# A last product with its weights stationary: the output of an MLP made transposed and turned by VectorE

## The chip, the cores and the metric

The kernel runs on one core of a Trainium2 chip. The metric is the device time of one execution in microseconds; for a kernel it is the median of its runs. Beside it stands one profiled execution, from which all rows below are read.

## The reference

The inputs `u`, `v` (4 x 3072 x 256) and `z` (4 x 3072 x 64) pass three stages; all arrays are float32.

```python
scores = (1.0 / S) * np.matmul(z, z.transpose(0, 2, 1))
attn_out = u * np.matmul(np.maximum(scores, 0.0) ** 2, v)
x_prev = np.concatenate([zeros((B, 1, D)), x[:, :-1]], axis=1)   # x = attn_out
xk = mu_k * x + (1.0 - mu_k) * x_prev
xr = mu_r * x + (1.0 - mu_r) * x_prev
k = np.maximum(xk @ w_k, 0.0)                  # 256 -> 1024
x2 = sigmoid(xr @ w_r) * (k * k @ w_v)         # 1024 -> 256
h = np.maximum(x2 @ w_in, 0.0)                 # 256 -> 2048
out = (h * h) @ w_out                          # 2048 -> 256, 12288 tokens
```

## The kernel before

Every float32 product is made of three matmuls on float32r parts: an operand is split into a high part (the value cast) and a low part (the rest), and high x high, low x high and high x low are summed in PSUM. The helper `split` (lines 80 to 85) makes the parts: the cast on ScalarE or VectorE, the subtraction on VectorE.

The first part, `attention`, takes some 1000 us. It makes the attention output for 24 blocks of 512 tokens and leaves it transposed (features on partitions, tokens along the columns) in DRAM, and between its steps it converts and stages the weights. The second part, `channel_mix_and_mlp`, goes over the 24 token blocks (`NBLK`), and it is the part that the change touches. Its order of work is written out by hand: for each of the 16 hidden chunks `f` of 128 features of a block (`NF2`), `up2` of the next chunk, a piece of the next block's first MLP (`up1`, `down1`, `gate_r`, from the table `before`), then `down2(n, f)`, then what the tables `after` and `aside` put there (mixing, gating, the load of a later x). After the sixteenth chunk comes `store(n)`. Each engine runs its instructions in this order, and so does SP with its transfers.

`up` (line 203) makes six matmuls for one chunk: 128 x 128 weights stationary, 512 tokens moving, three products for each half of the 256 inputs. ScalarE then takes relu and square (lines 157 and 158), VectorE the cast and the subtraction (84 and 85). `down1` (lines 218 to 222) also keeps the weights stationary: two accumulators of [128 features, 512 tokens], six matmuls a chunk.

`down2` (lines 524 to 533) does it the other way. The activations of 128 tokens are stationary, four times a chunk, and the weights move: once 512 columns (high and low part of `w_out` side by side, line 530), once 256 columns (the low part of the activations times the high part of the weights, line 532). The output then has tokens on partitions. It lies in four PSUM tiles `o0` to `o3` of one bank each, in one buffer; in each the second half collects the two small products. `store` adds the halves (ScalarE copies one, line 540, VectorE adds, line 541), and one transfer a block writes 512 KB (line 545; two of half the size in the last block). `split_piece` splits the pieces of `w_in` and `w_out` during the first block.

PSUM has eight banks: two for `ps_v`, four for `ps_o`, two for `ps_u`, whose two tiles `ups` are written by `up` and freed by the relu.

Of the kernel before, what the change touches and what calls it, by code (L numbers as in the profile page):

```python
# [7 lines left out]
F32 = mybir.dt.float32  # L8
F32R = mybir.dt.float32r
U32 = mybir.dt.uint32  # L10
AF = mybir.ActivationFunctionType
ALU = mybir.AluOpType
PSUM = bass.MemoryType.PSUM
DRAM = bass.MemoryType.DRAM

P = 128
Q = 32
T = 512
# [3 lines left out]
def tile_relu2_attention__rwkv_channel_mix__relu2_mlp(  # L22
# [18 lines left out]
    nc = tc.nc  # L41
    B, S, D = u.shape
# [3 lines left out]
    ND = D // P  # L46
    NJ = S // P
    NB = S // T
    NBLK = B * NB
    NF1 = F1 // P  # L50
    NF2 = F2 // P


    HS = 2.0**32
    G = 4
# [9 lines left out]
    raw_p = ctx.enter_context(tc.tile_pool(name="raw", bufs=3))  # L65
# [14 lines left out]
    def split(hi, lo, src, on_act=False):  # L80
        if on_act:
            nc.scalar.copy(hi, src)
        else:
            nc.vector.tensor_copy(hi, src)  # L84
        nc.vector.tensor_tensor(out=lo, in0=src, in1=hi, op=ALU.subtract)  # L85

    raws = {}
# [6 lines left out]
    def split_raw(key, hi, lo):  # L94
        split(hi, lo, raws.pop(key), True)
# [65 lines left out]
    def relu2_split(ps, scale):  # L161
        hi, lo = parts(*pools["hidden"])
        split(hi, lo, relu2(ps, scale))
        return hi, lo
# [32 lines left out]
    def up(lhs, rhs, f):  # L197

        ps = pools["ps"].tile([P, T], F32, tag="w", name="ups")
        k = 0  # L200
        for h, m in ((0, 0), (1, 0), (0, 1)):
            for c in range(ND):
                nc.tensor.matmul(ps, lhsT=lhs(h, c, f), rhs=rhs[:, m, c, :],  # L203
                                 start=k == 0, stop=k == 3 * ND - 1)
                k += 1
        return ps

    def up1(n, f):
        ps = up(lambda h, c, f: wk[:, h, c, f * P:(f + 1) * P], xk_t[n], f)
        kt[n, f] = relu2_split(ps, 1.0)  # L210
# [16 lines left out]
    def load_piece(i):  # L227
        if i < len(w_pieces):
            src = w_pieces[i][0]
            load_raw(("w32", i), src, src.shape[1], src.shape[2])  # L230
# [265 lines left out]
    def channel_mix_and_mlp():  # L496
        with ExitStack() as st:
            wp = st.enter_context(tc.tile_pool(name="wp", bufs=1, reuse_waits="tile"))
            ps_o = st.enter_context(tc.tile_pool(name="ps_o", bufs=1, space=PSUM, reuse_waits="tile"))
            ps_w = st.enter_context(tc.tile_pool(name="ps_u", bufs=2, space=PSUM, reuse_waits="tile"))  # L500
            win = [wp.tile([P, 2, ND, T], F32R, name=f"win{i}") for i in range(F2 // T)]
            wout = [wp.tile([P, G, 2, D], F32R, name=f"wout{i}") for i in range(NF2 // G)]
            pools["ps"], pools["hidden"] = ps_w, (wp, "h", 6)
            gt, acc_o, x2, sig = {}, {}, {}, {}

            def gate_r(n, d):
                ps = up(lambda h, c, f: wr[:, h, c, f * P:(f + 1) * P], xr_t[n], d)
                t = wp.tile([P, T], F32, tag=f"sig{d}", name="sig")
                nc.scalar.activation(out=t, in_=ps, func=AF.Sigmoid)
                sig[n, d] = t  # L510

            def gate_v(n, d):
                if d == 0:
                    x2[n] = wp.tile([P, 2, ND, T], F32R, tag="x2", name="x2", bufs=2)
                t = el.tile([P, T], F32, tag="a", name="x2f")
                nc.vector.tensor_tensor(out=t, in0=acc_v[n][d], in1=sig.pop((n, d)), op=ALU.mult)
                split(x2[n][:, 0, d, :], x2[n][:, 1, d, :], t)

            def up2(n, f):
                q, r = divmod(f, T // P)  # L520
                ps = up(lambda h, c, f: win[q][:, h, c, r * P:(r + 1) * P], x2[n], f)
                gt[n, f] = relu2_split(ps, HS)

            def down2(n, f):
                if f == 0:
                    acc_o[n] = [ps_o.tile([P, 2, D], F32, tag=f"o{c}", name=f"o{c}") for c in range(G)]
                hi, lo = gt.pop((n, f))
                w = wout[f // G]
                for c in range(G):
                    nc.tensor.matmul(acc_o[n][c], lhsT=hi[:, c * P:(c + 1) * P], rhs=w[:, f % G, :, :],  # L530
                                     start=f == 0, stop=False)
                    nc.tensor.matmul(acc_o[n][c][:, 1, :], lhsT=lo[:, c * P:(c + 1) * P], rhs=w[:, f % G, 0, :],  # L532
                                     start=False, stop=f == NF2 - 1)

            def store(n):
                y = raw_p.tile([P, G, D], F32, tag="raw", name="y")
                a = acc_o.pop(n)
                for c in range(G):
                    t = wp.tile([P, D], F32, tag="yc", name="yc", bufs=4)
                    nc.scalar.mul(t, a[c][:, 1, :], HS**-2)  # L540
                    nc.vector.scalar_tensor_tensor(out=y[:, c, :], in0=a[c][:, 0, :], scalar=HS**-2, in1=t,
                                                   op0=ALU.mult, op1=ALU.add)
                    if c == G - 1 or n == NBLK - 1 and c % 2:
                        c0 = c - 1 if n == NBLK - 1 else 0
                        nc.sync.dma_start(out=out[n * T + c0 * P:n * T + (c + 1) * P, :].rearrange("(c p) d -> p c d", p=P),
                                          in_=y[:, c0:c + 1])

            def split_piece(i):
                _, cs, fs = w_pieces[i]
                if i % 2 == 0:  # L550
                    t = win[fs.start // T]
                    split_raw(("w32", i), t[:, 0, cs], t[:, 1, cs])
                else:
                    t = wout[cs.start // G]
                    split_raw(("w32", i), t[:, :, 0, fs], t[:, :, 1, fs])
                load_piece(i + AHEAD)

            before, after, aside = {}, {}, {}  # L560
            for f, unit, a in ((0, up1, 2), (1, down1, 1), (2, up1, 3), (3, down1, 2), (4, up1, 4), (5, down1, 3),
                               (6, up1, 5), (7, down1, 4), (8, up1, 6), (9, down1, 5), (10, gate_r, 0),
                               (11, gate_r, 1), (12, down1, 7)):
                before[f] = (1, unit, a)
            after[9] = (1, up1, 7)
            after[10] = (1, down1, 6)
            before[13], before[14] = (2, up1, 0), (2, up1, 1)
            before[15] = (2, down1, 0)
            aside[1], aside[2] = (1, mix, 1, 0), (1, mix, 1, 1)
            aside[3] = (2, load_x)  # L570
            aside[7], aside[9] = (2, mix, 0, 0), (2, mix, 0, 1)
            aside[12], aside[13] = (1, gate_v, 0), (1, gate_v, 1)
            assert NF1 == 8 and NF2 == 16

            def run(n, what):
                if what and n + what[0] < NBLK:
                    what[1](n + what[0], *what[2:])

            gate_r(0, 0)
            gate_v(0, 0)  # L580
            split_piece(0)
            gate_r(0, 1)
            gate_v(0, 1)
            split_piece(1)
            up1(1, 0)
            up1(1, 1)
            up2(0, 0)
            up1(1, 2)
            for n in range(NBLK):
                last = n == NBLK - 1  # L590
                for f in range(NF2):
                    if f == 0 and last:
                        up2(n, 1)
                    ahead = n * NF2 + f + (2 if last else 1)
                    if ahead < NBLK * NF2:
                        up2(*divmod(ahead, NF2))
                    run(n, before.get(f) if n or f else (1, down1, 0))
                    down2(n, f)
                    run(n, after.get(f))
                    run(n, aside.get(f))  # L600
                    if n == 0 and f % 4 < 2 and f // 4 < 3:
                        split_piece(2 + f // 4 * 2 + f % 4)
                store(n)

    with tc.manual_schedule():
        attention()
        channel_mix_and_mlp()
# [29 lines left out]
```

## Time and profile before

| | |
|---|---|
| median of 3 runs | 2641.64 us (2640.64 to 2646.01) |
| the profiled execution | 2645.41 us, span 2643.6 us |
| TensorE busy | 2609.6 us, 99% of the span |
| VectorE busy | 1765.4 us, 67% |
| ScalarE busy | 1523.5 us, 58% |
| mean granted TensorE clock | 0.997 |

Busy times of TensorE come from records that overlap, since matmuls are pipelined and their ends are modelled: 99% says that something was always under way, not that the array was always full. The shares are means over the whole program. From about 1010 us on only the second part runs; there VectorE and ScalarE are busy for some 55% and 50% of the time.

### The profile page before, as it was taken

What the parts mean: (1) busy time and instruction counts of PE and PEld (TensorE: products, weight loads), DVE (VectorE), ACT (ScalarE), POOL (GpSimd) and SP (SyncE); (2) the same over time, 40 slices, a digit from 0 to 9 for tenths busy, and PEclk for the clock granted to TensorE, in tenths of its full rate; (3) what the DMA queues carried; (4) which work ended last, traced back from release to release, by engine and by line L of the source; (5) the groups of instructions that cost most, each with busy time, mean ns of one, the idle gap of its engine ahead of it and who ended that gap; (6) DMA issues with size and microseconds to landing.
All of it is one profiled execution on the core that took longest, in us unless ns stands there. A gap on an engine that the chain in (4) does not pass through costs nothing.

```text
span 2643.6 us, 33655 instructions
## 1 busy us (share of the span) xinstructions
PE 2609.6 (99%) x12096; PEld 2167.0 (82%) x12096; DVE 1765.4 (67%) x3118; ACT 1523.5 (58%) x2571; POOL 0.2 (0%) x4
## 2 busy tenths in 40 slices
PE   7999999999999999999999999999999999999999
PEld 6887888788788888888888888888888888888887
DVE  8887888888888886555555555555555555555554
ACT  8766876776577665454445554544544444455454
POOL 0000000000000000000000000000000000000000
PEclk9999999999999999999999999999999999999999
DMA  7687678776876752000000000000000000000000
GB/s 191 166 210 175 181 199 193 189 212 174 219 215 167 223 156 64 17 17 17 17 17 17 17 17 17 10 16 17 17 17 9 17 17 17 17 17 16 17 9 17
DMA packets 262952, 218.75 MB, mean 83 GB/s; under 512 B 160128, under 2 KB 190848, under 8 KB 259712
## 3 DMA queue, kind: packets, MB, share of 16 engines
q1 hardware_dynamic: 262784, 216.60, 30.2%
q8 instruction: 94, 1.54, 0.2%
q14 instruction: 74, 0.61, 0.1%
HBM read 124.28 MB, written 92.27 MB: 82 GB/s over the span
## 4 chain that ended last, share of the span: by engine, by line
PE 92%; DVE 3%; DMA 2%; SPq 1%; issue 1%; ACT 1%; DVEq 0%; ACTq 0%
PE ups L203 32%; PE o L530 13%; PE v L375 8%; PE v L371 8%; PE v L372 8%; PE o L532 7%; PE v L219 3%; PE v L222 3%; PE v L218 3%; PE sps L344 2%; PE sps L343 2%; DMA mixed<-turned 2%; SPq L245 1%; DVE alo L353 1%; DMA zn<-in_z_dram 1%
## 5 line engine op out<-in xcount | busy, mean ns | idle before, releaser
L157 ACT ACTIVATE a<-ups 128x512 f32<-128x512 f32 x576 | 344.1, 597 | 794.1 <-PE ups L203 778.2
L84 DVE CAST hhi<-a 128x512 fp32r<-128x512 f32 x568 | 242.2, 426 | 661.5 <-ACT a L158 646.0
L203 PE MATMUL ups<-x,win 128*128 128x512 f32 x2304 | 593.8, 393 | 0.5 <-DVE x L84 0.5
L158 ACT ACTIVATE a<-a 128x512 f32<-128x512 f32 x912 | 576.6, 632 | 29.1
L530 PE MATMUL o<-wout,hhi 128*128 128x512 f32 x1536 | 556.4, 397 | 0.0
L203 PEld LDWEIGHTS ups<-x,win 128*128 128x128 f32 x2304 | 408.6, 188 | 86.6 <-DVE x L84 0.9
L371 PE MATMUL v<-ahi,vhl 128*128 128x512 f32 x1152 | 451.3, 392 | 6.5 <-ACT ahi L338 6.4
L372 PE MATMUL v<-ahi,vhl 128*128 128x512 f32 x1152 | 451.0, 391 | 3.4 <-DVE vhl L278 3.4
L532 PE MATMUL o<-wout,hlo 128*128 128x256 f32 x1536 | 430.6, 280 | 0.0
L85 DVE TENSOR_TENSOR hlo<-a,hhi 128x512 fp32r<-128x512 f32 x568 | 393.5, 693 | 49.7 <-DVE hhi L84 2.3
L375 PE MATMUL v<-alo,vhl 128*128 128x512 f32 x1152 | 359.6, 394 | 12.4 <-DVE alo L353 12.2
L530 PEld LDWEIGHTS o<-wout,hhi 128*128 128x128 f32 x1536 | 288.8, 188 | 66.1
L532 PEld LDWEIGHTS o<-wout,hlo 128*128 128x128 f32 x1536 | 290.2, 189 | 14.8
L203 PE MATMUL ups<-mixed,wk 128*128 128x512 f32 x1152 | 292.9, 390 | 0.0
L375 PEld LDWEIGHTS v<-alo,vhl 128*128 128x128 f32 x1152 | 215.5, 189 | 65.2 <-DVE alo L353 20.3
L371 PEld LDWEIGHTS v<-ahi,vhl 128*128 128x128 f32 x1152 | 217.3, 189 | 54.6 <-ACT ahi L338 8.8
L372 PEld LDWEIGHTS v<-ahi,vhl 128*128 128x128 f32 x1152 | 217.6, 189 | 49.0 <-DVE vhl L278 3.7
L203 PEld LDWEIGHTS ups<-mixed,wk 128*128 128x128 f32 x1152 | 214.7, 188 | 45.3
L157 ACT ACTIVATE a<-sps 128x512 f32<-128x512 f32 x336 | 199.4, 594 | 81.4 <-PE sps L344 74.1
L314 DVE STREAM_TRANSPOSE turn<-a 128x512 f32<-128x512 f32 x240 | 207.9, 866 | 22.0 <-ACT a L158 21.6
L353 DVE TENSOR_TENSOR alo<-a,ahi 128x512 fp32r<-128x512 f32 x336 | 221.5, 664 | 0.0
L338 ACT CAST ahi<-mixed 128x512 fp32r<-128x512 f32 x220 | 132.2, 619 | 152.9 <-PE v L372 75.5
(69 smaller groups left out, 2281.5 us busy)
## 6 DMA issues: line engine op xcount, KB each, us to landing
turned<-turn SPq DMA_DIRECT2D x60, 1024.0 KB, 5.1
mixed<-turned SPq DMA_DIRECT2D x220, 256.0 KB, 5.3
raw<-in_v_dram SPq DMA_DIRECT2D x24, 512.0 KB, 5.2
u<-in_u_dram SPq DMA_DIRECT2D x192, 64.0 KB, 4.2
xT<-uT SPq DMA_DIRECT2D x48, 256.0 KB, 3.4
out_dram<-y SPq DMA_DIRECT2D x23, 512.0 KB, 2.9
x<-xT SPq DMA_DIRECT2D x20, 513.0 KB, 3.8
zn<-in_z_dram SPq DMA_DIRECT2D x96, 64.0 KB, 4.2
```

Of the source, the lines that this page charges most:

```text
L84: nc.vector.tensor_copy(hi, src)
L85: nc.vector.tensor_tensor(out=lo, in0=src, in1=hi, op=ALU.subtract)
L157: nc.scalar.activation(out=a, in_=ps, func=AF.Relu, scale=scale)
L158: nc.scalar.activation(out=a, in_=a, func=AF.Square)
L203: nc.tensor.matmul(ps, lhsT=lhs(h, c, f), rhs=rhs[:, m, c, :], start=k == 0, stop=k == 3 * ND - 1)
L314: nc.vector.transpose(t[:, :, :, c, :], a.rearrange("x (m r q) -> x q m r" if s else "x (m q r) -> x q m r", m=G, q=R))
L353: finish(lambda: nc.vector.tensor_tensor(out=lo, in0=a, in1=hi, op=ALU.subtract))
L371: nc.tensor.matmul(acc[n][d], lhsT=vt[:, 0, c, ds_], rhs=hi, start=first, stop=False)
L372: nc.tensor.matmul(acc[n][d], lhsT=vt[:, 1, c, ds_], rhs=hi, start=False, stop=False)
L375: nc.tensor.matmul(acc[n][d], lhsT=vt[:, 0, c, ds_], rhs=lo, start=False, stop=last)
L530: nc.tensor.matmul(acc_o[n][c], lhsT=hi[:, c * P:(c + 1) * P], rhs=w[:, f % G, :, :], start=f == 0, stop=False)
L532: nc.tensor.matmul(acc_o[n][c][:, 1, :], lhsT=lo[:, c * P:(c + 1) * P], rhs=w[:, f % G, 0, :], start=False, stop=f == NF2 - 1)
```

## The change

`down2` keeps a 128 x 128 tile of `w_out` stationary and moves the activations of 512 tokens. It has two accumulators (one for each half of the 256 output features), each of one bank and in two buffers, and makes six matmuls a chunk in place of eight. The output now has features on partitions. `store` scales each accumulator on ScalarE, transposes it on VectorE in blocks of 32 x 32 and writes it with four transfers a block, one from each group of 32 partitions, in pieces of 64 contiguous floats; in the last block every other of them is issued by ScalarE. So that a transposed block holds neighbouring features, `split_piece` permutes the columns of `w_out`: each of its four pieces is split in two steps, one for each half.

```diff
-            ps_o = st.enter_context(tc.tile_pool(name="ps_o", bufs=1, space=PSUM, reuse_waits="tile"))
+            ps_o = st.enter_context(tc.tile_pool(name="ps_o", bufs=2, space=PSUM, reuse_waits="tile"))
...
-            wout = [wp.tile([P, G, 2, D], F32R, name=f"wout{i}") for i in range(NF2 // G)]
+            wout = [wp.tile([P, 2, G, D], F32R, name=f"wout{i}") for i in range(NF2 // G)]
...
             def down2(n, f):
                 if f == 0:
-                    acc_o[n] = [ps_o.tile([P, 2, D], F32, tag=f"o{c}", name=f"o{c}") for c in range(G)]
+                    acc_o[n] = [ps_o.tile([P, T], F32, tag=f"o{d}", name=f"o{d}") for d in range(ND)]
                 hi, lo = gt.pop((n, f))
-                w = wout[f // G]
-                for c in range(G):
-                    nc.tensor.matmul(acc_o[n][c], lhsT=hi[:, c * P:(c + 1) * P], rhs=w[:, f % G, :, :],
-                                     start=f == 0, stop=False)
-                    nc.tensor.matmul(acc_o[n][c][:, 1, :], lhsT=lo[:, c * P:(c + 1) * P], rhs=w[:, f % G, 0, :],
-                                     start=False, stop=f == NF2 - 1)
+                w, c = wout[f // G], f % G
+                for d in range(ND):
+                    ds_ = slice(d * P, (d + 1) * P)
+                    nc.tensor.matmul(acc_o[n][d], lhsT=w[:, 0, c, ds_], rhs=hi, start=f == 0, stop=False)
+                    nc.tensor.matmul(acc_o[n][d], lhsT=w[:, 1, c, ds_], rhs=hi, start=False, stop=False)
+                for d in range(ND):
+                    ds_ = slice(d * P, (d + 1) * P)
+                    nc.tensor.matmul(acc_o[n][d], lhsT=w[:, 0, c, ds_], rhs=lo, start=False, stop=f == NF2 - 1)
 
             def store(n):
-                y = raw_p.tile([P, G, D], F32, tag="raw", name="y")
+
+                y = raw_p.tile([P, T // Q, ND, Q], F32, tag="raw", name="y")
                 a = acc_o.pop(n)
-                for c in range(G):
-                    t = wp.tile([P, D], F32, tag="yc", name="yc", bufs=4)
-                    nc.scalar.mul(t, a[c][:, 1, :], HS**-2)
-                    nc.vector.scalar_tensor_tensor(out=y[:, c, :], in0=a[c][:, 0, :], scalar=HS**-2, in1=t,
-                                                   op0=ALU.mult, op1=ALU.add)
-                    if c == G - 1 or n == NBLK - 1 and c % 2:
-                        c0 = c - 1 if n == NBLK - 1 else 0
-                        nc.sync.dma_start(out=out[n * T + c0 * P:n * T + (c + 1) * P, :].rearrange("(c p) d -> p c d", p=P),
-                                          in_=y[:, c0:c + 1])
+                for d in range(ND):
+                    t = wp.tile([P, T], F32, tag="yT", name="yT", bufs=2)
+                    nc.scalar.mul(t, a[d], HS**-2)
+                    nc.vector.transpose(y[:, :, d, :], t.rearrange("x (k q) -> x k q", q=Q))
+                w = ND * Q
+                for p in range(P // Q):
+                    e = nc.scalar if n == NBLK - 1 and p % 2 else nc.sync
+                    e.dma_start(out=out[n * T:(n + 1) * T, p * w:(p + 1) * w].rearrange("(k q) f -> q k f", q=Q),
+                                in_=y[p * Q:(p + 1) * Q].rearrange("q k d r -> q k (d r)"))
...
                     t = wout[cs.start // G]
-                    split_raw(("w32", i), t[:, :, 0, fs], t[:, :, 1, fs])
+
+                    src = raws.pop(("w32", i)).rearrange("x c (p d r) -> x c p d r", d=ND, r=Q)
+                    for d in range(ND):
+                        split(*(t[:, h, :, d * P:(d + 1) * P].rearrange("x c (p r) -> x c p r", r=Q) for h in range(2)),
+                              src[:, :, :, d], True)
```

## Rows read from the trace of the kernel before

**Rows 1.** The page: TensorE's busy time, and the granted clock in 40 slices.
```profile
PE 2609.6 (99%) x12096; PEld 2167.0 (82%) x12096; DVE 1765.4 (67%) x3118; ACT 1523.5 (58%) x2571; POOL 0.2 (0%) x4
...
PEclk9999999999999999999999999999999999999999
```

**Rows 2.** Waits, 1014.6 to 2639 us: who waited for whom, us, times, longest.
```profile
ACT a L157 <- PE ups L203: 767.3, 381, 3.5
DVE hhi L84 <- ACT a L158: 646.0, 379, 4.3
...
DVE hlo L85 <- PE o L532: 0.5, 1, 0.5
```

**Rows 3.** Timeline (start, us, engine): first of 24 matmuls without a break, and the next.
```profile
997.53 0.39 PE L371 MATMUL v<-ahi,vhl 128*128 128x512 f32 x1
...
1002.97 2.88 PE L203 MATMUL ups<-mixed,wr 128*128 128x512 f32 x12
```

**Rows 4.** Timeline: the output's evacuation of two blocks, one block lying between.
```profile
1149.16 1.44 ACT L540 ACTIVATE yc<-o 128x256 f32<-128x256 f32 x4 [0.44 <-PE o L532]
...
1287.30 1.44 ACT L540 ACTIVATE yc<-o 128x256 f32<-128x256 f32 x4 [0.44 <-PE o L532]
```

**Rows 5.** The chain's end (start, us, what): first and eleventh of the up-products.
```profile
2606.23 1.38 PE ups L203 x6
...
2634.09 1.39 PE ups L203 x6
```

**Rows 6.** Timeline: one group of the last product and what follows it.
```profile
2554.83 0.39 PE L530 MATMUL o<-wout,hhi 128*128 128x512 f32 x1
...
2555.06 0.28 PE L532 MATMUL o<-wout,hlo 128*128 128x256 f32 x1
...
2555.17 0.40 PE L530 MATMUL o<-wout,hhi 128*128 128x512 f32 x1
...
2556.24 1.55 PE L203 MATMUL ups<-x,win 128*128 128x512 f32 x6
```

**Rows 7.** Tile and line views: durations in ns, min/median/max, first and last start.
```profile
L157 ACT ACTIVATE a<-ups x576: 577/598/612, 955.6 to 2635.5; 128x512 f32<-128x512 f32 x192
...
L290 DVE STREAM_TRANSPOSE uT<-u x48: 669/704/766, 43.5 to 991.8; 128x512 f32<-128x512 f32 x48
...
L314 DVE STREAM_TRANSPOSE turn<-a x240: 668/711/1159, 21.4 to 943.2; 128x512 f32<-128x512 f32 x120
```

**Rows 8.** Timeline at a block boundary; idle before and releaser in brackets.
```profile
1079.56 0.39 PE L530 MATMUL o<-wout,hhi 128*128 128x512 f32 x1
...
1082.54 0.60 ACT L157 ACTIVATE a<-ups 128x512 f32<-128x512 f32 x1 [1.00 <-PE ups L203]
...
1083.84 0.43 DVE L84 CAST hhi<-a 128x512 fp32r<-128x512 f32 x1 [1.59 <-ACT a L158]
...
1085.10 1.55 PE L203 MATMUL ups<-x,win 128*128 128x512 f32 x6
```

**Rows 9.** Transfers: issues 0 to 12; queue 0 to 6, 2598 to 2604; landing, last block.
```profile
0.73 4.10 SPq L245 DMA_DIRECT2D zn<-in_z_dram  x8
...
q1 hardware_dynamic: 4151, 0.52, 53.1%
...
q1 hardware_dynamic: 528, 0.52, 25.9%
...
out_dram<-y SPq DMA_DIRECT2D x2, 256.0 KB, 2.2
```

**Rows 10.** Timeline: the cast of a w_out piece; the page: a cast of 512 columns.
```profile
1006.45 1.05 ACT L82 CAST wout<-raw 128x1024 fp32r<-128x1024 f32 x1
...
L338 ACT CAST ahi<-mixed 128x512 fp32r<-128x512 f32 x220 | 132.2, 619 | 152.9 <-PE v L372 75.5
```

**Rows 11.** The end: the last group's first matmul; the stores, first and last start.
```profile
2638.12 0.40 PE L530 MATMUL o<-wout,hhi 128*128 128x512 f32 x1
...
L545 SPq DMA_DIRECT2D out_dram<-y x25: 372/377/378, 1082.3 to 2640.6; - x25
```

## The prediction, made before the result was known

> **What bounds the kernel now.** I read the page first: TensorE is busy 99% of the span and the granted clock stands at the top digit in all forty slices [rows 1], which is the upper level of 2.4 GHz. A busy TensorE can still be waiting, so the list of waits came next, from the first matmul of the last product to the end [rows 2]: the long ones are ScalarE and VectorE waiting for TensorE's results, and no row has TensorE itself as the one that waits. So in this part of the kernel the time is the number of matmuls times their spacing, and the other engines and the stores matter only where they hold TensorE up, or after its last matmul.
>
> The recorded durations (about 390 ns for 512 columns) overlap, so I price by distance from start to start. In the timeline 24 matmuls of 512 columns run without a break from 997.53 to 1002.97 [rows 3]: 5.44 / 24 = 0.2267 us each. These are the products of the attention and of the first layer, which already have the form that the changed product gets: weights or values stationary, activations moving, three matmuls for each half of the output.
>
> One token block of the MLP stage makes, by the code, 8 x 6 (up1) + 8 x 6 (down1) + 2 x 6 (gate) + 16 x 6 (up2) = 204 matmuls of 512 columns, and 16 x 8 = 128 of the last product. The evacuation of the output comes once per block, at 1149.16 and, two blocks later, at 1287.30 [rows 4]: 69.07 us a block. Less 204 x 0.2267 = 46.24 that leaves 22.83 us for 16 groups of the last product, **1.427 us a group**. The tail of the last block, where only up2 and down2 alternate, gives a second reading: in the chain, ten rounds from 2606.23 to 2634.09 [rows 5] are 2.786 us each, less 6 x 0.2267 = 1.360, so 1.426. The two agree.
>
> **The matmuls, before and after.** A group before is four pairs of a 512-column matmul and a 256-column one; after, six of 512. The columns are the same: 4 x 768 = 3072 = 6 x 512. What differs is the spacing. In one group the 512-column matmul starts at 2554.83, the 256-column one 0.23 later and the next 512-column one 0.11 after that; the six matmuls that follow the group start at 2556.24, so the pairs alone take 1.41 [rows 6]. The rest up to 1.427 is paid by the first matmul behind the group. The new group has the form of rows 3: 6 x 0.2267 = 1.360. Saved: 1.427 - 1.360 = 0.067 us a group, and 24 blocks x 16 = 384 groups give **25.6 us**. Bounds: hundredth-of-a-microsecond stamps leave 0.062 to 0.072 (23.8 to 27.6); if what the pairs leave to the following matmul were not theirs, 1.41 - 1.36 = 0.05, or 19.2.
>
> The trace and a page part here. By rows 3 and 4 a full matmul costs 0.2267 and a pair 1.427 / 4 = 0.357, which is 0.017 more than the one and a half matmuls that its columns make. The Trainium skill (TensorE: Matmul & The Clock Gate, Back-to-back issue gap) gives N / 2.4 GHz plus about 2.5 ns for an isolated matmul, so by it a group would go from 1.300 to 1.295 us and the change would save an estimated 2 us in all; the trace has both forms wider apart, and unevenly. The sum goes by the rows.
>
> **The output accumulators.** They become two tiles of one bank with two buffers each instead of four with one. TensorE waits for none of them now (no such row in rows 2), so the second buffer gives nothing.
>
> **The evacuation at each block boundary.** Before: four ScalarE copies and four VectorE multiply-adds of 256 columns. After: two copies and two transposes of 512. A ScalarE pass of that size over PSUM is 0.60 us, the nearest transposes take 0.70 plain and 0.71 with blocks scattered, 1.16 at worst [rows 7]. The copies can start only when the fifth of the six matmuls is through. With the group starting at 1079.56, the fifth starts at +0.91, its record (0.39) ends at +1.30, the copies run from about +1.34 to +2.54 (1082.10) and the transposes end at about +3.40 (1082.96). ScalarE's next work waits for TensorE until 1082.54, VectorE's next is at 1083.84 [rows 8]. Both fit: zero cost, covered by these gaps. Without the gaps the next things late would be the release of the up-product's PSUM bank, wanted at 1085.10, and then the cast behind it.
>
> The store becomes four transfers from 32 partitions, in 256-byte pieces: per block 2048 packets in place of 512. They lie beside 68 us of matmuls. Issuing four takes SP about 4 x 0.51 us, by the eight issues of the same 32-partition shape at the start [rows 9]. Behind them in SP's queue stands the next load of x, which is wanted some twenty microseconds later; nothing waits.
>
> **The weights' split** for w_out (four pieces) goes from one 1024-column cast of 1.05 us and one subtraction to two of each at half size: 2 x 0.62, the price of a 512-column cast [rows 10], is 0.2 us more each on ScalarE and about as much on VectorE, all during the first block, where both have idle time. Zero; 0.8 us if that cover were gone.
>
> **The end of the program**, counted from the start of the last group (2638.12 before). Before: the last store is issued at +2.48 (2640.6) and lands 2.2 us later, +4.7 [rows 9, 11]. After: copies from +1.34, first transpose +1.95 to +2.70, second to +3.40, since both halves are needed by each of the four stores. They are issued on two queues, the second of each about 0.5 later. How long 2048 packets of 256 bytes take is not in the trace. From below, packets of about 125 bytes: 53.1% of 16 engines over 6 us for 4151 of them, 12.3 ns each. From above, packets of 1 KB: 25.9% of 16 x 6 us for 528, 47 ns [rows 9]. A straight line between them puts 256 bytes at 17 ns; nearest is the small row. 128 packets per engine then take 2.2 us (1.6 to 6.0). Of the 2.2 us of a landing now, 16 packets x 47 ns make 0.8 of data, so 1.4 are fixed; the later issues lie under the data of the first. They land at 3.45 + 1.4 + 2.2 = +7.05: **2.3 us later** than before (1.6 to 7, the upper end with slow transposes too).
>
> The Trainium skill (DMA: Bandwidth & Descriptors, Specifications) says that pieces under 512 bytes make the engines read, modify and write, which speaks against these stores; no store of so small a piece is in this trace, and my upper end of 47 ns a packet stands without that rule.
>
> **Sum.** Against the profiled execution's own 2645.41 us (span 2643.6 and 1.8 around it): -25.6 + 2.3 = -23.3, so 2622.1. That execution lies 3.8 above the median of the runs, 2641.64; on the median the forecast is **2618.3**. Bounds: -27.6 + 1.6 = -26 (2615.6) and -19.2 + 7 = -12.2 (2629.4).
>
> **Rivals.**
> *Columns alone.* TensorE's time would follow columns, and the 0.067 us of a group would belong to its place in the stage and not to the narrow matmuls. Then only the end changes: +2.3, 2643.9. For it: the column counts are equal. Against it: up1, down1 and up2 stand in the same stage beside the same work and fit 0.2267. Chance 4%.
> *The stores eat the gain at the end.* If the 32-partition stores ran on a quarter of the engines, 512 packets each at 47 ns make 24 us, and the gain is gone: 2618.3 + 22 = 2640; at twice the upper price on all engines, 12 us, it would be 2628. Against the first: the loads of that shape at the start keep 53% of all 16 engines busy, their first microsecond without data included. Chance 5%, mostly for the milder form.
> *A new wait at the block boundary*, the one that ends on the slow side. The copies now begin 0.8 us later in the group, and if ScalarE or VectorE came so late that the up-product's bank is not free at 1085.10, TensorE would stop at each of 23 boundaries. It decides from 23.3 / 23 = 1.0 us of stall each. ScalarE's release comes at 1083.14 now [rows 8], so it has 1.96 us of room plus 0.44 before that; the copies would have to end 3.4 us later than worked out. A stall of 2 us would give 2618.3 + 46 = 2664. Chance 4%.
> The forecast has 87%.
>
> A measurement of this kernel tells about 0.2% (5.3 us) from no change. Faster by more: the forecast, and the milder half of the stores rival and a little besides, 0.91. Within: columns alone and the harder stores, 0.05. Slower: the boundary, 0.04. The range, 2614 to 2628, takes in the bounds of the matmul saving and of the end but for their extreme sum, and a microsecond or two between runs.
>
> **What would show it.** Right: evacuations 68.0 us apart instead of 69.07; the six matmuls of a group 0.227 apart and the up-product behind them no longer stretched; no wait with TensorE as the waiting engine; transposes of 0.70 to 0.75 us; the last store landing about 7 us after the last group's start. Wrong: matmuls of the new group 0.238 apart (columns alone), a long gap after the last transpose (stores), or TensorE waiting at the boundary behind ScalarE. The forecast fails above all if the new group's two accumulators, each written twice in a row, space the matmuls wider than the same order does in down1.

## The result, and the profile after

The changed kernel takes 2619.87 us in the median of four runs (2617.43 to 2622.30); the kernel before, in four, 2642.03. The ratio is 0.9914 with a 95% interval from 0.9897 to 0.9931, so it is faster by 0.9%, more than the 0.2% that a measurement of this kernel can tell. Forecast were 2618.3 us and a range from 2614 to 2628. The median fell by 22.2 us, and 23.3 had been forecast. Execution against execution: the profiled one went from 2645.41 to 2622.30 us, and 2622.1 had been worked out for it; that these agree to 0.2 us is partly luck, as the division below shows.

The page after, TensorE's busy time and its granted clock, answers to [rows 1].
```profile
PE 2580.9 (98%) x11328; PEld 2126.1 (81%) x11328; DVE 1764.8 (67%) x3074; ACT 1515.2 (58%) x2527; POOL 0.2 (0%) x4
...
PEclk9999999999999999999999999999999999999999
```
There are 768 matmuls fewer (384 groups x 2). The busy share tells nothing of the gain: TensorE was full before and is full after, with less to do.

The waits of the changed kernel from 1014.6 to 2616 us (who waited for whom, us, times, longest), beside [rows 2]:
```profile
ACT a L157 <- PE ups L203: 731.9, 381, 3.5
DVE hhi L84 <- ACT a L158: 602.5, 357, 4.2
ACT yT L543 <- PE o L535: 29.7, 23, 2.6
DVE y L544 <- ACT yT L543: 15.3, 23, 2.0
```
Again no row has TensorE as the waiting engine. What is new are ScalarE's waits for the end of a group and VectorE's for the copy, once at each of 23 of the blocks' ends: they are idle time of engines that had it to spare.

The timeline around one group of the changed kernel, and the copies of two blocks, two blocks apart; they answer to [rows 6] and [rows 4].
```profile
1146.99 1.09 ACT L543 ACTIVATE yT<-o 128x512 f32<-128x512 f32 x2 [1.23 <-PE o L535]
...
1282.99 1.09 ACT L543 ACTIVATE yT<-o 128x512 f32<-128x512 f32 x2 [1.23 <-PE o L535]
...
2526.05 0.39 PE L531 MATMUL o<-hhi,wout 128*128 128x512 f32 x1
...
2527.41 1.52 PE L203 MATMUL ups<-x,win 128*128 128x512 f32 x6
2528.77 0.39 PE L218 MATMUL v<-hhi,wv 128*128 128x512 f32 x1
```
A group lasts 2527.41 - 2526.05 = 1.36, and the six up-products behind it 1.36 too, where they took 1.38 to 1.39 before [rows 5]. The blocks are (1282.99 - 1146.99) / 2 = 68.00 us apart in place of 69.07.

In the chain's end after, for [rows 5], ten rounds of up-product and group run from 2580.61 to 2607.81: 2.720 us each, twice 1.360.

The end after, in the timeline, for [rows 11]:
```profile
2611.73 0.39 PE L531 MATMUL o<-hhi,wout 128*128 128x512 f32 x1
...
2613.06 1.08 ACT L543 ACTIVATE yT<-o 128x512 f32<-128x512 f32 x2 [2.59 <-PE o L535]
2613.69 1.30 DVE L544 STREAM_TRANSPOSE y<-yT 128x512 f32<-128x512 f32 x2 [1.97 <-ACT yT L543]
2615.03 0.85 SPq L548 DMA_DIRECT2D out_dram<-y  x2
2615.03 0.93 ACTq L548 DMA_DIRECT2D out_dram<-y  x2
```
And its transfers, 2608 to 2621 us (queue, packets, MB, share of 16 engines):
```profile
q10 hardware_dynamic: 1056, 0.26, 12.6%
q1 hardware_dynamic: 1056, 0.26, 11.8%
```
The copies start 1.33 us after the last group's first matmul and the stores are issued at +3.30. The span ends at 2620.5, +8.77; before it ended at 2643.6 - 2638.12 = +5.48.

So the 23.1 us between the two spans divide into three: from the first group's start to the last one's 25.5 (2638.12 - 1014.64 = 1623.48 before, 2611.73 - 1013.73 = 1598.00 after), 0.9 because this execution reached the first group earlier (1013.73 against 1014.64; nothing ahead of it was changed but the split of one piece, and among the fourteen profiled executions this start lies anywhere from 1010.5 to 1014.6, so it is chance), and the end, which gives 3.3 back. The end is 1.0 us dearer than forecast, and the chance gain of 0.9 hides it in the comparison of the two executions.

### The profile page after: what moved, and what is told of

Same layout as the page of the kernel before. It is cut to its first block, busy times and chain, and to the rows that moved or that the text cites. A ratio compares the mean times of both kernels' runs of the same rounds, so it can differ in the third digit from the quotient of the medians.

```text
span 2620.5 us, 32286 instructions
## 1 busy us (share of the span) xinstructions
PE 2580.9 (98%) x11328; PEld 2126.1 (81%) x11328; DVE 1764.8 (67%) x3074; ACT 1515.2 (58%) x2527; POOL 0.2 (0%) x4
## 4 chain that ended last, share of the span: by engine, by line
PE 91%; DMA 3%; DVE 3%; SPq 2%; ACT 1%; issue 1%; DVEq 0%; ACTq 0%
PE ups L203 32%; PE v L375 8%; PE v L371 8%; PE v L372 8%; PE o L531 7%; PE o L532 7%; PE o L535 7%; PE v L218 3%; PE v L222 3%; PE v L219 3%; PE sps L344 2%; PE sps L343 2%; DMA mixed<-turned 2%; SPq L245 1%; DMA zn<-in_z_dram 1%
## 5 line engine op out<-in xcount | busy, mean ns | idle before, releaser
L203 PE MATMUL ups<-x,win 128*128 128x512 f32 x2304 | 584.7, 389 | 0.5 <-DVE x L84 0.5
L203 PEld LDWEIGHTS ups<-x,win 128*128 128x128 f32 x2304 | 432.4, 188 | 90.7 <-DVE x L84 0.9
L375 PE MATMUL v<-alo,vhl 128*128 128x512 f32 x1152 | 358.0, 392 | 14.6 <-DVE alo L353 13.7
L531 PE MATMUL o<-hhi,wout 128*128 128x512 f32 x768 | 298.8, 389 | 0.0
L532 PE MATMUL o<-hhi,wout 128*128 128x512 f32 x768 | 298.8, 389 | 0.0
L375 PEld LDWEIGHTS v<-alo,vhl 128*128 128x128 f32 x1152 | 214.5, 188 | 67.5 <-DVE alo L353 23.1
L535 PE MATMUL o<-hlo,wout 128*128 128x512 f32 x768 | 236.4, 389 | 0.0
L339 DVE TENSOR_TENSOR alo<-mixed,ahi 128x512 fp32r<-128x512 f32 x220 | 146.3, 690 | 41.7 <-ACT ahi L338 40.5
```

The source lines that it names most:

```text
L375: nc.tensor.matmul(acc[n][d], lhsT=vt[:, 0, c, ds_], rhs=lo, start=False, stop=last)
L531: nc.tensor.matmul(acc_o[n][d], lhsT=w[:, 0, c, ds_], rhs=hi, start=f == 0, stop=False)
L532: nc.tensor.matmul(acc_o[n][d], lhsT=w[:, 1, c, ds_], rhs=hi, start=False, stop=False)
L535: nc.tensor.matmul(acc_o[n][d], lhsT=w[:, 0, c, ds_], rhs=lo, start=False, stop=f == NF2 - 1)
```

## The experiments

All are variants of the changed kernel but the third. "Group" is one chunk of the last product; its time is read from the distance between the copies of consecutive blocks, less 204 x 0.2267 us, over 16.

**Narrow matmuls put back, weights still stationary.** The low part's product is halved and the halves are set between the wide matmuls.
```diff
-                    nc.tensor.matmul(acc_o[n][d], lhsT=w[:, 0, c, ds_], rhs=hi, start=f == 0, stop=False)
-                    nc.tensor.matmul(acc_o[n][d], lhsT=w[:, 1, c, ds_], rhs=hi, start=False, stop=False)
...
+                    for h in range(2):
+                        hs = slice(h * T // 2, (h + 1) * T // 2)
+                        nc.tensor.matmul(acc_o[n][d], lhsT=w[:, h, c, ds_], rhs=hi, start=f == 0 and h == 0, stop=False)
+                        nc.tensor.matmul(acc_o[n][d][:, hs], lhsT=w[:, 0, c, ds_], rhs=lo[:, hs],
+                                         start=False, stop=f == NF2 - 1 and h == 1)
```


> The changed kernel, but the product with the low part of the activations is made in two halves of 256 columns each, set between the 512-column matmuls, so that a group has the four pairs of 512 and 256 columns of the kernel before while the weights stay stationary. Same columns, same result. Theory (the narrow matmuls cost the time): a group goes back to 1.427 us, evacuations 69.07 us apart, and all of the 25.6 us comes back: 2619.9 + 25.6 = 2645. Rival 1 (each matmul has a fixed price, 226.7 less the 213.3 ns of 512 columns at 2.4 GHz, 13 ns): two more matmuls a group, 384 x 2 x 0.0134 = 10 us, 2630. Rival 2 (what mattered was which operand is stationary): a group stays at 1.36, 2620.

Measured: 2648.13 us, ratio 1.0017 (1.0007 to 1.0026) to the kernel before. The timeline, two blocks' copies and one group:
```profile
1149.11 1.31 ACT L543 ACTIVATE yT<-o 128x512 f32<-128x512 f32 x2 [0.79 <-PE o L534]
...
1287.24 1.31 ACT L543 ACTIVATE yT<-o 128x512 f32<-128x512 f32 x2 [0.79 <-PE o L534]
...
2525.40 0.39 PE L533 MATMUL o<-hhi,wout 128*128 128x512 f32 x1
2525.63 0.28 PE L534 MATMUL o<-hlo,wout 128*128 128x256 f32 x1
2525.74 0.40 PE L533 MATMUL o<-hhi,wout 128*128 128x512 f32 x1
```
69.07 us a block, to the hundredth what the kernel before had: the shape alone brings the whole cost back, with 0.23 and 0.11 between the starts as in [rows 6]. What is stationary does not matter. The kernel ends a little behind the one before because it keeps the longer end.

**The four narrow ones together, behind the wide ones.** The same matmuls, with the loop over the halves of the low part moved behind both halves' wide ones.

> As the run with alternating halves, but the four 256-column matmuls of a group stand together behind the four of 512. Theory (a matmul behind a narrow one pays, some 0.017 us each, since its weight load has only the narrow one's time to lie under): four matmuls still follow a narrow one, so 1.43 a group and 2645 or a little more. Variant of the theory: if consecutive loads bind, the narrow ones follow each other at up to the 0.188 us that a load's record lasts, 0.91 + 0.75 = 1.66 a group, 2735. Rival (fixed price a matmul): 2630.

Measured: 2639.56 us, ratio 0.9985 (0.9975 to 0.9994). Timeline:
```profile
1146.29 1.09 ACT L546 ACTIVATE yT<-o 128x512 f32<-128x512 f32 x2 [1.24 <-PE o L537]
...
1283.78 1.09 ACT L546 ACTIVATE yT<-o 128x512 f32<-128x512 f32 x2 [1.24 <-PE o L537]
...
2528.14 1.07 PE L532 MATMUL o<-hhi,wout 128*128 128x512 f32 x4
2529.04 0.64 PE L537 MATMUL o<-hlo,wout 128*128 128x256 f32 x4
2529.51 1.55 PE L203 MATMUL ups<-x,win 128*128 128x512 f32 x6
2530.90 1.29 PE L203 MATMUL ups<-mixed,wk 128*128 128x512 f32 x5
```
68.745 us a block, 1.407 a group. Neither account had it: the theory, by which every matmul behind a narrow one pays, said 1.43 or more, the fixed price alone 1.387. Four narrow ones take 2529.51 - 2529.04 = 0.47, about 0.118 each, little more than half a wide one; the six wide ones behind them take 1.39 in place of 1.36. Two windows of the same timeline that begin later (a window leaves out what has ended before it) give the second and the sixth of these six:
```profile
2529.75 1.32 PE L203 MATMUL ups<-x,win 128*128 128x512 f32 x5
...
2530.68 0.39 PE L203 MATMUL ups<-x,win 128*128 128x512 f32 x1
```
The first takes 0.24, the first five 2530.68 - 2529.51 = 1.17 in place of 1.13, the sixth 0.22. So the delay is not one matmul's: over some 350 groups of this trace the five stand on average 233, 236, 228, 232 and 231 ns apart, and those behind them 227. The four narrow ones take 113, 119, 120 and 120 ns.

**The kernel before with wide matmuls only.** The 256-column matmul is widened to 512 and so also adds the product of the two low parts.
```diff
-                    nc.tensor.matmul(acc_o[n][c][:, 1, :], lhsT=lo[:, c * P:(c + 1) * P], rhs=w[:, f % G, 0, :],
+                    nc.tensor.matmul(acc_o[n][c], lhsT=lo[:, c * P:(c + 1) * P], rhs=w[:, f % G, :, :],
```


> The kernel before (activations stationary, weights moving), with the matmul of 256 columns widened to 512: it also adds the product of the two low parts. Eight full matmuls a group. Theory (form of the operands is free, only narrow matmuls are dear): 8 x 0.2267 = 1.813 a group, 384 x (1.813 - 1.427) = 148 us over the kernel before, 2790. Rival 2 (activations as the stationary operand cost 0.017 us a pair by themselves): 1.88 a group, 2816.

Measured: 2793.5 us, ratio 1.0566 (1.0545 to 1.0587). The copies in its timeline:
```profile
1082.98 1.75 ACT L540 ACTIVATE yc<-o 128x256 f32<-128x256 f32 x4 [0.55 <-PE o L532]
1158.23 1.75 ACT L540 ACTIVATE yc<-o 128x256 f32<-128x256 f32 x4 [0.55 <-PE o L532]
```
75.25 us a block: (75.25 - 46.24) / 16 = 1.813 a group, eight times 0.2267. With activations stationary a wide matmul costs what it costs everywhere. The same 0.067 us could have been lost to the operands' roles; it is not.

**Only narrow matmuls.** Every matmul of a group in two halves.

> The changed kernel with every matmul of a group in two halves of 256 columns: twelve narrow ones in place of six wide (eleven in the first group of a block, whose first matmul stays wide). So far: four wide and four narrow alternating make a group of 1.427 us, four wide and then four narrow 1.406; there the narrow ones stand 0.1175 apart and the six up-products behind them take 1.385 in place of 1.36. Account A (a narrow matmul costs half the columns plus a fixed 0.009 us, and the first wide one behind narrow ones 0.027): 12 x 0.1175 + 0.027 = 1.44 a group, 384 x 0.08 = 30 us over the changed kernel, 2651. Account B (each extra matmul 0.020, each wide one behind a narrow one 0.007, the other way to solve the two runs): 1.36 + 0.12 + 0.007 = 1.487, 49 us, 2669. Account C (weight loads of 0.188 bind when all are narrow): 12 x 0.188 = 2.26, 345 us, 2965.

Measured: 2656.94 us, ratio 1.0053 (1.0036 to 1.0070).
```profile
1146.55 1.32 ACT L544 ACTIVATE yT<-o 128x512 f32<-128x512 f32 x2 [0.81 <-PE o L535]
...
1285.69 1.32 ACT L544 ACTIVATE yT<-o 128x512 f32<-128x512 f32 x2 [0.81 <-PE o L535]
...
2520.38 0.64 PE L535 MATMUL o<-hhi,wout 128*128 128x256 f32 x4
2520.85 0.40 PE L535 MATMUL o<-hlo,wout 128*128 128x256 f32 x2
2521.09 0.64 PE L535 MATMUL o<-hhi,wout 128*128 128x256 f32 x4
2521.57 0.40 PE L535 MATMUL o<-hlo,wout 128*128 128x256 f32 x2
2521.81 1.55 PE L203 MATMUL ups<-x,win 128*128 128x512 f32 x6
2523.20 0.39 PE L218 MATMUL v<-hhi,wv 128*128 128x512 f32 x1
```
A block takes 69.57 us and a group 1.458. Twelve narrow matmuls take 2521.81 - 2520.38 = 1.43 and the six wide ones behind them 1.39. Account A is nearest, with a fixed price that was set too low; C falls, so that the weight loads' records of 0.188 us are no bound on the spacing. The first four narrow ones take 0.47, as in the run with the narrow ones last; the eight behind them take 2521.81 - 2520.85 = 0.96, 0.120 each, where half a wide one is 0.1133. If a matmul costs so much a column and something that does not depend on its width, the second part is 2 x 0.120 - 0.2267 = 0.0133 us, a **fixed price** for each matmul, and the first is 0.417 ns a column, one cycle at the clock's upper level of 2.4 GHz. Every matmul here has a weight load of its own, so the runs do not tell whose price it is.

**The narrow ones first.** The four narrow matmuls open the group.

> The four narrow matmuls of a group stand first and the four wide ones behind them (in the first group of a block, which must open with a wide one, they stand last). The count and the number of wide matmuls behind a narrow one are those of the run with the narrow ones last. Theory (what follows a narrow matmul pays, wherever that is): 1.406 a group, 2639, and now the up-product behind the group takes 1.36 again while the four wide ones are stretched. Rival (the up-product itself is what was delayed, by its own operands): 1.38 a group, 2630.

Measured: 2641.0 us, ratio 0.9992 (0.9982 to 1.0002); 68.745 us a block again (the copies of two blocks stand at 1145.26 and 1282.75).
```profile
2527.30 0.64 PE L535 MATMUL o<-hlo,wout 128*128 128x256 f32 x4
2527.77 1.09 PE L535 MATMUL o<-hhi,wout 128*128 128x512 f32 x4
2528.70 1.53 PE L203 MATMUL ups<-x,win 128*128 128x512 f32 x6
2530.07 1.52 PE L203 MATMUL ups<-mixed,wk 128*128 128x512 f32 x6
```
The stretch has moved with the narrow ones: the four wide ones take 2528.70 - 2527.77 = 0.93 in place of 0.907, the up-products 1.37. It belongs to the wide matmuls that follow a narrow one, wherever they stand.

Put together, over a group of six wide matmuls:

| arrangement | over 1.360 | extra matmuls x 0.0133 | rest | changes from narrow to wide |
|---|---|---|---|---|
| four wide, four narrow, alternating (before, and put back) | 0.067 | 2: 0.027 | 0.040 | four, 0.010 each |
| narrow together, last or first | 0.047 | 2: 0.027 | 0.020 | one |
| all narrow | 0.098 | 6: 0.080 | 0.018 | one |

Behind a run of narrow matmuls the change costs about 0.02 us, whether the run has four or twelve.

**One buffer for the accumulators** (`bufs=1` for `ps_o`).

> The changed kernel with one buffer for the output accumulators in place of two. Theory (the second buffer gives nothing): the copies end about 2.4 us after the last group starts and the next block's first group starts 4.1 us after it, so TensorE waits for nothing and the time is that of the changed kernel, 2620 within the runs' spread. Rival (the second buffer hides a wait): 23 boundaries, a stall that shows as a wait of the first matmul of a group for the copy; at 0.5 us each 2631.

Measured: 2621.29 us, ratio 0.9915 (0.9900 to 0.9930), 68.00 us a block, no wait of TensorE. The second buffer gives nothing, as forecast.

**More copies at the boundary.**
```diff
+                spare = wp.tile([P, T], F32, tag="spare", name="spare")
+                for _ in range(4 if n < NBLK - 1 else 0):     # 10 in the second kernel
+                    nc.scalar.mul(spare, a[d], HS**-2)
```


> The changed kernel, with four more ScalarE copies of an accumulator into a spare tile behind the two copies of each block but the last: 4 x 0.55 = 2.2 us of ScalarE at each of 23 boundaries. It tests the room at the boundary. In the changed kernel's trace the copies end 2.43 us after the last group's start, ScalarE is idle for 0.50 us, and the relu then ends 1.9 us before the up-product needs its bank: 2.4 us of room. Theory: 2.2 fits, 2620 and no wait of TensorE. Rival (the boundary is already tight): each copy costs its time, 23 x 2.2 = 50 us, 2670.

> The same with ten more copies, 5.5 us a boundary. Theory: 3.1 us over the room of 2.4, so TensorE waits 3.1 us at each of 23 boundaries, 71 us: 2691, with the wait in the up-product's matmul for the relu. Rival (there is far more room, since the schedule runs ahead): 2620. Rival (no room): 127 us, 2747.

Four copies: 2621.51 us, ratio 0.9916 (0.9896 to 0.9936). The waits of that kernel now have a row of TensorE's weight load:
```profile
PEld ups L203 <- ACT a L157: 3.8, 23, 0.2
```
3.8 us in 23 boundaries, at most 0.2: the room of 2.4 us is just used up, and the block has grown to 68.03. Ten copies: 2741.29 us, ratio 1.0369 (1.0348 to 1.0390), some 50 more than expected. Its timeline at two boundaries, and its windows (engines' busy time with counts, then the granted clock, DMA share, GB/s):
```profile
1079.36 6.27 ACT L547 ACTIVATE spare<-o 128x512 f32<-128x512 f32 x10
...
1086.17 1.92 PE L203 MATMUL ups<-x,win 128*128 128x512 f32 x6 [3.52 <-ACT a L157]
...
1088.31 0.63 PE L219 MATMUL v<-hhi,wv 128*128 128x512 f32 x1
...
1088.74 0.63 PE L218 MATMUL v<-hhi,wv 128*128 128x512 f32 x1
...
1518.35 1.09 ACT L543 ACTIVATE yT<-o 128x512 f32<-128x512 f32 x2 [1.23 <-PE o L535]
...
1526.14 1.66 PE L203 MATMUL ups<-x,win 128*128 128x512 f32 x6 [3.52 <-ACT a L157]
...
1590.18 1.09 ACT L543 ACTIVATE yT<-o 128x512 f32<-128x512 f32 x2 [1.23 <-PE o L535]
...
1663.64 1.09 ACT L543 ACTIVATE yT<-o 128x512 f32<-128x512 f32 x2 [1.23 <-PE o L535]
```
```profile
1088.00:1090.40 2.40, 2.40 (x7) 1.87 (x6) 1.97 (x5) 1.84 (x3) 0.00 (x0) 0.50 0.00 0
1092.00:1110.00 18.00, 18.00 (x81) 14.89 (x80) 8.89 (x16) 8.09 (x14) 0.00 (x0) 1.00 0.09 30
...
1526.10:1531.10 5.00, 4.96 (x22) 4.09 (x23) 3.97 (x8) 3.53 (x6) 0.00 (x0) 1.00 0.00 0
```
The wait came where it was expected, at the up-product's bank, and each of the 23 stalls of TensorE is 3.52 us long, not 3.1, for the ten copies take 6.27 us and not 5.5. But behind 19 of them the clock is granted at 0.50, and matmuls stand 0.43 apart in place of 0.2267; behind the other four, that of 1526.14 among them, it stays at 1.00, after a stall of the same length. A block with such a stall alone takes 1590.18 - 1518.35 = 71.83 us, 3.83 over the changed kernel; with the slow stretch behind it, as in the next block, 73.46 (73.2 to 73.5 in the others). So the slower clock costs 1.3 to 1.6 us where it comes. Of the 50 us over the forecast the longer stalls make 23 x (3.83 - 3.1), about 17, and the clock 19 x 1.5, about 28. What decides whether the clock falls behind a stall these runs do not show.

**Stores in pieces of 128 bytes.** Each of the four stores of a block is made in two, one for each half of the features.

> The changed kernel with each store split in two, of 128-byte pieces: eight transfers a block and 4096 packets in place of 2048. Theory (stores are hidden except the last): the evacuations stay 68.0 us apart; at the end 256 packets an engine in place of 128. At the 12 ns of the 128-byte loads they would take about as long as now (3.1 against the 24 ns x 132 = 3.2 of the changed kernel), at 24 ns twice as long, and four issues a queue in place of two add about 1 us: the span's end 1 to 4 us later, 2621 to 2624. Rival (small stores cost the stage too, through DMA or SP): some tens of us, growing with the packets.

Measured: 2620.4 us, ratio 0.9912 (0.9897 to 0.9927). Its last group starts at 2608.53 and its span ends at 2617.5: +8.97, only 0.2 later with twice the packets, where 1 to 4 had been expected; the blocks stay 68.00 us apart. The queue lines of its last 13 us, 2608 to 2621:
```profile
q10 hardware_dynamic: 2112, 0.26, 14.1%
q1 hardware_dynamic: 2112, 0.26, 13.8%
```
27.9% of 16 x 13 us for 4224 packets is 13.7 ns each. Small stores cost the stage nothing, and a packet of half the bytes takes little more than half the time.

**The last block as before.** The last block is computed with activations stationary and stored in rows of 1 KB; eight additions of 128 columns undo the permutation.

> The changed kernel, but its last block is computed and stored as in the kernel before (activations stationary, eight matmuls a group, stores of 1 KB rows, four copies and eight half-size additions that undo the permutation). Theory (the changed kernel's end is 3.3 us longer for the late transposes and the small packets): 16 x 0.067 = 1.07 us more in the block, and the end, from the last group's start, goes from 8.8 back to about 6.1 us: the span 1.5 us shorter than the changed kernel's, which only the profile can show. Rival (the end is fixed cost): 1 us longer.

> The changed kernel itself, for a measurement on the same chip as the run below: 2620, 0.991 to 0.992 of the kernel before.

> The kernel whose last block is made and stored as before, again, with more rounds beside the changed kernel. Theory: 1.6 us faster than the changed kernel (2.7 at the end, less 1.07 in the block), 0.06%, which is at the edge of what five rounds can tell; the profile's end, from the last group's start, 6.1 us against 8.8.

Measured: 2619.23 us, ratio 0.9904 (0.9888 to 0.9921), and again 2620.04, ratio 0.9909 (0.9894 to 0.9924); the changed kernel beside the second 2619.8, ratio 0.9911 (0.9896 to 0.9926). Its last group started at 2613.09 and its span ended at 2619.2, +6.1 as expected; in the second profile 2611.82 and 2619.1, +7.3, since there the last stores took 3.6 us to land and not 2.2. With 1.07 us paid in the block, 0.4 to 1.6 us remain, which the runs do not show. It is no version to prefer.

## Why the prediction was right

*The matmuls.* 25.6 us were forecast for 384 groups (25.7 by the forecast's own terms), 25.5 were measured over the 383 between the first group's start and the last one's. The price of the new group was taken from matmuls of the same form shortly ahead of the stage, and it came out at that price, 1.360. What the forecast did not know was where the 0.067 us come from. Ten microseconds (384 x 2 x 0.0133) are the fixed price of two matmuls, the other fifteen come with the changes from narrow to wide. That this stretch fell partly on the up-product behind the group, as read from [rows 6], the run with the narrow ones first showed; but it is not paid by the first matmul there, as the prediction has it, but shared by the first five. Why wide matmuls are stretched is not settled: the weights of the first were loaded while a narrow one ran, but the stream of narrow ones, whose loads all have that little time, is not slowed in the same measure.

*Columns alone.* Falls: with equal columns the groups measured 1.360, 1.407, 1.427 and 1.458. The Trainium skill (TensorE: Matmul & The Clock Gate, Back-to-back issue gap) adds about 2.5 ns to an isolated matmul's columns; here the two widths give 13 ns, and a rule of columns and one constant has no place for the stretch. The measurement decides.

*The boundary.* Zero was forecast, on gaps of ScalarE and VectorE. The copies ended 2.4 us after the group's start (2.54 forecast), and the room until TensorE stops, 2.4 us, was confirmed by the run whose four copies took 2.50 us and cost a block 0.03. The rival's condition was placed rightly, but its price was too low: it counted the stall and not the clock, which fell behind 19 of 23 stalls of 3.52 us. It would have decided from less than 1.0 us a boundary only if a shorter stall also lowered the clock, which no run shows.

*The end.* 2.3 us were forecast, 3.3 measured. The step that was mis-sized is the time of a packet of 256 bytes: 17 ns by the line between two sizes, while 24.4% of 16 x 13 us for 2112 packets is 24 ns. 132 x 24 = 3.2 us of data stand in place of 2.2. The other times hold: copies at +1.33 (1.34 forecast), stores issued at +3.30 (3.45). It lay within the bounds, and the rival in which the stores eat the gain falls. The Trainium skill (DMA: Bandwidth & Descriptors, Specifications) gives a threshold of 512 bytes below which a write is also read; the runs show 47 [rows 9], 24 and 13.7 ns for packets of 1024, 256 and 128 bytes, so a byte in small packets is dearer, about twofold, but between 256 and 128 hardly further. Whether the packets were read back no run here shows.

*The accumulators and the weights' split.* Nothing for either, as forecast; for the split there is only the absence of a new wait.

## What to carry to other kernels

Where TensorE is full, price a change of form by the distance from start to start of matmuls of that form in the same trace, over a whole period of the schedule: a single group's rows left out what the narrow matmuls did to the work behind them. At equal columns, fewer and equally wide matmuls win, and where narrow ones can't be avoided, they cost less together than in between wide ones. An engine beside a full TensorE has room up to a point that can be read from the gaps; beyond it the price can be more than the stall.

## What the runs showed of the hardware

Behind 19 of 23 stalls of 3.52 us TensorE's clock was granted at 0.50, the lower of its two levels (1.2 GHz of 2.4), in a stretch in which matmuls already ran again; behind the other four, of the same length, it stayed at 1.00. A block lost 3.83 us with the stall alone and 5.2 to 5.5 with both. In a row a matmul of 512 columns, with its weight load, takes 0.2267 us and one of 256 columns 0.120, so 0.0133 of either does not depend on the width. A change from narrow to wide costs 0.010 us more in alternation and about 0.02 behind a run of four or twelve narrow ones, and there the first five wide ones share it. And stores of 128-byte pieces from 32 partitions moved nearly as many bytes in a microsecond as those of 256: 13.7 ns a packet against 24.
